# A new instruction order for an adaLN transformer block with local dilated attention and a token-mixing MLP, with the condition first on ScalarE's queue

## The chip, the cores and the metric

The kernel runs on one core of one Trainium2 chip. A core has five engines, each with its own instruction queue worked in order: TensorE (PE, matmuls; PEld is its weight load), VectorE (DVE), ScalarE (ACT), GpSimd (POOL) and SyncE (SP, which here only issues DMA). ACT can issue DMA too. The engines meet at semaphores. The metric is the device time of one execution in microseconds (us).

## What is computed

The reference is one transformer block over 2048 tokens of width 512, modulated by one condition vector `c`:

```python
mod = (silu(c) @ w_mod)            # six rows of 512: sa, ca, ga, sb, cb, gb
h = layernorm(x) * (1 + ca) + sa
x = x + ga * attention(h, wqkv, wo)
h = layernorm(x) * (1 + cb) + sb
x = x + gb * token_mlp(h, w1, b1, w2, b2)
```

The attention has 32 heads of 16 columns. Each token looks at 8 keys at distances 0, 2, ..., 14 before it, and masked positions stand for keys before the first token. The MLP normalizes once more and then mixes along the token axis: `u = gelu(h^T w1 + b1)` with 1792 hidden units for each of the 512 columns, and `y = u w2 + b2` back to 2048 tokens.

## The kernel before

**Tiling.** The 2048 tokens are 16 tiles of 128. Attention goes over them in five chunks of 2, 4, 4, 4 and 2 tiles. In a chunk (function `build_chunk`, from line 616 on) each tile gets its first layernorm: statistics `ln1s`, variance `ln1v`, `rstd1` on ACT, `nb1` on DVE, normalization `n1`. The tiles are then transposed, for the first two chunks by PE (`tr`, with copies `hT` out of the accumulator), later by DMA (`xt`). Twelve or six matmul groups (`qkv`) form q, k and v, and copies (`ev`) take them out. DVE multiplies q with the shifted k (`qk`, one large product for each of four column groups), PE sums these over the head's columns (`red`), and a softmax follows: maximum on DVE (`max`), subtraction on PE (`sub`), exponential on ACT (`exp`), sum on PE (`esum`), reciprocal as two activations on ACT (`rcp`), scaling on DVE (`smB`). The weights are spread to other partitions by DMA (`a2`), v is copied to four shifted layouts by DMA (`vd`), DVE multiplies both (`pv`), PE sums (`pvacc`), ACT copies out (`oev`), and the output projection (`wo`) with the residual gives `x1`. The second layernorm (`ln2`, `n2`, `aff`) and the MLP's own (`ln3`, `h3`) close the chunk.

**The MLP.** The first matrix product (`mlp1`) accumulates over tokens as the chunks finish: for the hidden tiles 0 to 6 in three parts (tiles 0 to 5, 6 to 10, 11 to 15), for 7 to 13 in two (0 to 9, 10 to 15). Parts that are done are parked (`park`) and added back (`padd`), then `gelu` on ACT. The second product (`mlp2`) has 14 matmuls of 512 columns for each of the 16 output tiles; `fin` on DVE adds bias, gate and residual, and `st_out` stores.

**The condition.** `ld_c` loads the vector, PE transposes it with an identity matrix (`cps`), ACT and DVE form silu (`silu_exp`, `silu_dve`), and PE multiplies it with two blocks of `w_mod`: `modcols1` gives the columns of 1 + ca (`a1col`), `modcols0` those of sa (`sab`). `a1col` scales the transposed tokens of the first two chunks (`hT0`, `hT1`) and the qkv weights for the later ones (`wsc`). sa goes through the weights as a bias (`qvb`). The other four rows are formed by `modrow0` and `modrow1` and spread over all partitions by a store and a load (`st_row`, `ld_row`); `woq_s` scales the output projection with ga.

**What sets the order.** Nothing is left to a scheduler at run time. Each piece of work is a node (`add`, `add_any`) with one or more engines it may run on. The string `ORDER` (lines 191 to 249) lists all nodes by name. `schedule` (line 86) walks through it, takes for each node the engine that a suffix names (`:a` ACT, `:d` DVE, `:p` POOL, `:s` SP; on matmuls `:q` splits the stationary operand into four 32-column pieces, `:n` leaves out the matmul that would add a residual or a parked sum), gives it buffers from the pools, and emits its instructions in that order. So the string fixes each engine's instruction order, the order of each DMA queue, and which accumulator buffer each node gets.

**Idle matmuls.** A token `fill:N` emits matmuls of the identity with itself whose result nobody reads: N // 4 of 512 columns and N % 4 of 128 columns (`fill_fn`, line 528). They need only the identity, which POOL makes (`ident`, line 473; its last instruction, the memset of `epscol`, is the one PE waits for). POOL also zeroes the halo (`halo0`) and makes the other constants (`consts`, line 479).

**The names at the front.** `act_table` is ACT's load of its function table. `ld_x0` and `ld_x1` load the first two token tiles of 128 KB each, `ld_x_1_2` and `ld_x_1_4` two pairs of the second chunk, `ld_x_2_6` and `ld_x_2_8` two of the third. `ld_wmod1` and `ld_wmod0` load 512 KB each of `w_mod`, `ld_wqkv0` to `ld_wqkv2` the q, k and v weights. `dma2` (line 381) is a load that may be issued on SP or ACT; `ld_c` is a plain node of ACT in before (lines 429 and 430).

Of the kernel before, what the change touches and what calls it, by code (L numbers as in the profile page):

```python
# [196 lines left out]
qkv0_00 qvb0 wsc0_0:p ev0_10:a ld_b2 ld_wo1 hT1_1:d qkv1_00 ln1s11:d ln1s10:d ln1s13:d qkv1_10:q ln1v11 ln1v10  # L197
qvb_cp0:a ev0_00:a ln1s12:a ev0_02:d qkv1_13 ld_wqkv2 qkv0_20 ln1v13 qk0_3 qk0_2 ev1_13:a qk0_0 qvb1 ln1v12 qkv0_22:q
ld_wrow0 red0_0 ev1_00:a qkv1_03:q ev1_10:a qk0_1 red0_1 red0_2 red0_3 mask qvb_cp1:a ev0_20:a ev0_22:a wsc1_2:p
halo_v1:a qk1_0 ev1_03:a wsc1_3:a qkv1_11:q ld_wmod2 wsc2_3:a modrow0 ld_b1 mrows0:a ev1_11:a ld_wrow2 qkv1_02 max0  # L200
wsc0_2:p ld_wo0 n1_7:p sub0 rstd1_3 qkv1_01 ld_wo2 exp0 qkv1_12:q wsc1_1:p esum0:q qk1_3 red1_0 ev1_01:a qk1_1
ev1_02:a biascols n1_6:p ld_wrow1 rcp0 smB0 ev1_12:a ld_x_4_14 ln1s14:a qkv1_22 qk1_2 a2_0_2:a xt6 ld_wrow3 modrow1
red1_1 a2_0_1:a n1_9:p wsc2_0:d ln1s15:a ln1v14 nb1_3 n1_11:a qkv1_23:q mrows1 qkv1_21 ev1_21:a red1_2 red1_3 xt8
ev1_23:a fill:1 n1_10:p qkv1_20 ev1_20:a ev1_22:a qkv2_13 qkv2_10 wsc0_1:p vd0_2 ev2_13:a ln1v15 vd0_1 max1 sub1
qkv2_00 exp1 a2_0_0:s a2_0_3:s pv0_1 vd0_0 pv0_0 st_row0 pv0_2 qkv2_03 esum1:q ld_wo3 pvacc0_0 vd0_3 halo_v2:p
biascols_cp:a pvacc0_1 pv0_3 pvacc0_2 pvacc0_3 ev2_10:a ev2_00:a qk2_0 n1_13:a n1_12:a ld_row0 woq_s rcp1 smB1
oev0_2:a qkv2_11 qkv2_02:q ev2_03:a qk2_3 qkv2_01:q red2_0 oev0_0:a wo0:q wsc2_1:a wsc2_2:a qkv2_12 ev2_11:a ev2_01:a
ev2_02:a ev2_12:a wo1 qkv2_21:q a2_1_1:a qkv2_22 x1_1:a ln2q1:a x1_0:a xt10 ln2q0:a qk2_1 qkv2_23 xt12 qk2_2 a2_1_0:s
halo_k3:a ln2m0 vd1_2 a2_1_2:s qkv3_12 a2_1_3:s pv1_2 rstd1_4 red2_1 nb1_4 vd1_0 st_row1 red2_2 red2_3 rstd2_0
ev2_22:a nb2_0 ev2_21:a qkv3_13:q ev3_13:a max2 vd1_3 pv1_0 n1_14:a vd1_1 pvacc1_2 n1_15:a qkv2_20:q ev2_20:a sub2  # L210
qkv3_22:q ev3_12:a pv1_1 qkv3_10 exp2 ev2_23:a halo_v3:a qkv3_20 n2_0:a oev1_2:a ev3_10:a esum2 rcp2 qkv3_00 ev3_22:a
qkv3_02:q ev3_00:a pv1_3 ev3_02:a pvacc1_0 ev3_20:a qkv3_01:q ev3_01:a qkv3_11:q xt14 ld_row1 n2_1:p vd2_3 pvacc1_1
smB2 aff0 qk3_0 vd2_1 fill:1 vd2_0 oev1_0:a oev1_1:a pvacc1_3 ev3_11:a qk3_1 qkv3_23:q oev1_3:a a2_2_2:s ln3s1:a
qkv3_03:q wo4 a2_2_1:s qk3_2 a2_2_0:s ev3_03:a ev3_23:a x1_4:a ln2q4:a wo2 x1_2:a a2_2_3:s red3_0 wo3:q x1_3:a ln2q3:a
qkv3_21:q ev3_21:a wo5 red3_1 pv2_3 x1_5:a vd2_2 qk3_3 qkv4_20:q red3_2 qkv4_22 red3_3 qkv4_12 fill:18 ln2q5:a
ld_w1_0_512 ln2q2:a ln2m2 pv2_0 pvacc2_0 vd3_0 ev4_20:a ln3s0:a ln3v0 ev4_12:a rstd2_2 ev4_22:a ln3v1 qkv4_02 oev2_0:a
ln2m4 rstd2_4 nb2_2 n2_2:a max3 sub3:q exp3 pvacc2_3 oev2_3:a qkv4_10:q pv2_2 vd3_2 esum3 nb2_4 pv2_1 vd3_1 n2_3:p
ld_w1_0_0 n2_5:a rcp3 smB3 pvacc2_2 fill:14 a2_3_0:s a2_3_1:s a2_3_3:s n2_4:a qkv4_00:q oev2_2:a rstd3_0 aff2 pvacc2_1
oev2_1:a wo6 wo9 wo7 aff4 nb3_0 ln3s2:d ev4_02:a ln3s3:a ln3v3 h3_1:p wo8 a2_3_2:s ev4_00:a ln3v2 ld_w2_0 ln3s4:d
rstd3_2 nb3_2 x1_9:a ln3s5:a h3_0:p mlp1_0_6_0:q x1_7:a ln3v4 x1_8:a h3_3:d mlp1_0_1_0 h3_2:d mlp1_0_6_2 mlp1_0_1_2  # L220
pv3_1 mlp1_0_5_0:q ln3v5 ev4_10:a ld_w1_0_896 x1_6:a mlp1_0_3_0:q mlp1_0_3_2:q ln2q7:a pvacc3_1 rstd3_4 mlp1_0_5_2:q
oev3_1:a mlp1_0_2_0:q pv3_0 mlp1_0_2_2:q nb3_4 h3_4:a mlp1_0_0_0:q mlp1_0_0_2 h3_5:a mlp1_0_0_4:q qk4_0 ln2q8:a
ln2q6:a park0_0:a ln2q9:a mlp1_0_6_4:q mlp1_0_2_4:q mlp1_0_1_4:q park0_1:a pv3_2 mlp1_0_5_4:q vd3_3 pvacc3_0 oev3_0:a
mlp1_0_3_4:q ld_w2_1 park0_2:a pv3_3 red4_0 ln2m6 pvacc3_2 oev3_2:a mlp1_0_4_0:q qk4_1 pvacc3_3 ld_w1_0_1152
mlp1_0_4_2:q mlp1_0_4_4:q rstd2_6 oev3_3:a wo12:q halo_v4:p vd4_2 vd4_3 nb2_6 n2_9:a qk4_2 n2_7:d qk4_3 wo10:qn red4_1
ld_w1_0_1408 n2_6:a vd4_1 n2_8:a aff6 red4_2 red4_3 max4 park0_3:a ln3s8:d ln3s6:d x1_12:a ln3v8 wo11 vd4_0 ln3s9:d
mlp1_0_7_0 ld_w2_3 park0_4:a ln3v6 mlp1_0_7_2 park0_5:a ln3v9 x1_11:a ln2q12:a mlp1_0_8_0 mlp1_0_8_2 park0_6:a wo13:n
ln3s7:a ln3v7 sub4 mlp1_0_10_0 mlp1_0_9_0 x1_13:d exp4 rstd3_6 nb3_6 esum4 mlp1_0_8_4 ln2q13:a ln2m12 mlp1_0_10_2
mlp1_0_10_4 mlp1_0_9_2 rcp4 mlp1_0_7_4 h3_8:d rstd2_12 mlp1_0_12_0 mlp1_0_12_2 mlp1_0_12_4 smB4 a2_4_1:a a2_4_0:s
mlp1_0_9_4 a2_4_2:s h3_9:d a2_4_3:a h3_7:d nb2_12 h3_6:p mlp1_0_7_6 ln2q11:a park0_7:a x1_10:d mlp1_0_8_6 ld_w1_0_1664  # L230
ln2q10:a park0_8:a n2_13:p mlp1_0_9_6 park0_9:a n2_12:d aff12 ln2m10 rstd2_10 mlp1_0_10_6 park0_10:a ln3s13:a pv4_2
nb2_10 ld_w1_1_0 pv4_1 mlp1_0_11_0 mlp1_0_11_2 mlp1_0_11_4 mlp1_0_12_6 pv4_0 mlp1_0_11_6 ld_w1_1_640 inj1_6:qn pv4_3
pvacc4_0 pvacc4_1 n2_11:a mlp1_0_13_0:q pvacc4_2 pvacc4_3 n2_10:a mlp1_0_13_2:q park0_11:a mlp1_0_13_4 oev4_0:a
oev4_2:a aff10 ln3s10:a wo14 inj1_3:n ln3s11:d ln3v11 x1_14 ln2s14 wo15 x1_15 mlp1_0_13_6 ln2v14 ln3s12:a ln3v10
ln2s15 rstd2_14 nb2_14 ln2v15 n2_14:d rstd3_10 aff14 rstd2_15 nb2_15 inj1_4:qn ln3v13 park0_12:a mlp1_1_3_6 park0_13:a
mlp1_1_6_6 inj1_1:n mlp1_1_1_6 n2_15:p mlp1_1_4_6 inj1_0:n mlp1_1_0_6 nb3_10 h3_10:a mlp1_1_4_10 mlp1_1_3_10 ln3s14:d
# [839 lines left out]
```

## Time and profile before

| what | us |
|---|---|
| median of 3 runs | 201.37 |
| lowest, highest | 201.23, 201.57 |
| profiled execution, whole time | 202.11 |
| its span, first to last instruction | 200.4 |

The granted clock of TensorE is 1.00 over the span. The page slices the span into 40 parts of 5.01 us and gives each engine's busy share in tenths; the last digit for PE is 3 because the last output is formed and stored there:

```profile
PE   3999999999899999999999999999999999999993
PEld 1387754554344455534444444444444444444453
DVE  2689999999999999999999999986655253726554
ACT  4879897998899999999999698953670000000000
POOL 4155001200100001030000200320000000000000
```

PE's digit says that a matmul was in flight, not that it ran at its best pace: matmuls overlap, and one of 512 columns is in flight for 379 to 382 ns in most groups while the next starts behind it much sooner. DVE and ACT digits can be read as they stand. In a row of the timeline the first number is the start, the second the duration; the bracket tells how long the engine was idle before it and who ended that.

### The profile page before, as it was taken

The page shows a single profiled execution, that of the slowest core. Times are in us where ns is not written, and L with a number is a line of the kernel's source. Part 1 is how long each engine was busy: PE and PEld are TensorE (multiplying, and loading weights), DVE is VectorE, ACT ScalarE, POOL GpSimd, SP SyncE. Part 2 cuts the span into 40 slices and gives each one's busy share as a digit, 9 for nine tenths or more (in the row PEclk, how much of TensorE's full clock was granted, in tenths as well). Part 3 has the DMA queues.
Part 4 walks back from the last instruction along what each step waited for, and adds up shares of the span by engine and source line. Part 5 has one row for each costly group of instructions (what it writes and reads, how often), then busy time and mean ns, then how long its engine had stood idle before and what let it go on. Part 6 is the DMA issues. An engine that isn't in the chain of part 4 may idle for free.

```text
span 200.4 us, 4572 instructions
## 1 busy us (share of the span) xinstructions
PE 191.0 (95%) x1818; PEld 95.8 (48%) x1836; DVE 159.6 (80%) x241; ACT 128.6 (64%) x306; POOL 18.6 (9%) x45
## 2 busy tenths in 40 slices
PE   3999999999899999999999999999999999999993
PEld 1387754554344455534444444444444444444453
DVE  2689999999999999999999999986655253726554
ACT  4879897998899999999999698953670000000000
POOL 4155001200100001030000200320000000000000
PEclk9999999999999999999999999999999999999999
DMA  5999594826758745549399268568999201011611
GB/s 161 341 355 350 176 240 127 160 56 185 300 143 321 220 167 194 176 112 311 64 310 257 36 184 196 160 186 234 338 244 298 85 26 52 27 52 52 174 52 52
DMA packets 53889, 35.95 MB, mean 179 GB/s; under 512 B 24428, under 2 KB 50668, under 8 KB 53868
## 3 DMA queue, kind: packets, MB, share of 16 engines
q1 hardware_dynamic: 52228, 35.21, 61.2%
q10 hardware_dynamic: 1640, 0.46, 1.0%
q8 instruction: 14, 0.23, 0.5%
q14 instruction: 7, 0.06, 0.1%
HBM read 22.55 MB, written 2.10 MB: 123 GB/s over the span
## 4 chain that ended last, share of the span: by engine, by line
PE 69%; DVE 22%; issue 4%; DMA 1%; ACT 1%; ACTq 0%; DVEq 0%
PE psS L142 67%; DVE big L142 14%; PE psL L142 3%; DVE st L142 2%; DVE h L142 2%; DMA c_t<-in_c_dram 1%; DVE mv L142 1%; ACT h L142 1%; DVE lsb L142 1%; DVE m L142 1%; DVE nb L142 0%; ACTq L142 0%; DVE woq L142 0%; DVE hT L142 0%; ACT rb L142 0%
## 5 line engine op out<-in xcount | busy, mean ns | idle before, releaser
L142 PEld LDWEIGHTS <-wst 128*128 128x128 bf16 (+1 forms) x536 | 34.9, 101 | 33.7 <-issue 4.0
L142 PE MATMUL psS<-h,wst 128*128 128x512 bf16 (+1 forms) x333 | 50.3, 380 | 0.5 <-issue 0.3
L142 DVE TENSOR_TENSOR big<-q_sb,k_f 128x4096 bf16<-128x4096 bf16 (+1 forms) x20 | 36.6, 1859 | 0.4 <-ACT q_sb L142 0.4
L142 DVE TENSOR_TENSOR big<-a2sb,vD 128x4096 bf16<-128x4096 bf16 (+1 forms) x20 | 36.5, 1860 | 0.2
L142 PE MATMUL psS<-hT,w_qkv 128*32 128x512 bf16 (+3 forms) x360 | 29.7, 346 | 0.0
L142 DVE SCALAR_TENSOR_TENSOR h<-psS,bcol,rows_bc 128x512 f32<-128x512 f32 (+2 forms) x17 | 12.1, 710 | 22.1 <-PE psS L142 20.6
L142 PEld LDWEIGHTS <-w_qkv 128*32 128x32 bf16 (+1 forms) x402 | 19.4, 109 | 17.8 <-issue 4.4
L142 PE MATMUL psS<-gT,big 128*128 128x512 bf16 x110 | 24.7, 379 | 0.1
L142 PEld LDWEIGHTS <-big 128*128 128x128 bf16 x144 | 12.0, 97 | 13.5
L142 ACT ACTIVATE junk<-xx 128x512 bf16<-128x512 bf16 x26 | 16.3, 627 | 3.3 <-DVE xx L142 1.4
L142 PE MATMUL psS<-woq,o_sb 128*32 128x512 bf16 (+1 forms) x107 | 15.7, 380 | 0.9 <-ACT o_sb L142 0.6
L142 ACT ACTIVATE gT<-psS,bcol 128x512 bf16<-128x512 f32 x14 | 9.0, 685 | 8.1 <-DVE psS L142 8.0
L142 POOL TENSOR_SCALAR h<-xx,rs,nb 128x512 bf16<-128x512 bf16 x9 | 6.9, 766 | 75.6 <-DVE nb L142 36.5
L142 DVE TENSOR_TENSOR psS<-psS,gT 128x512 f32<-128x512 f32 x14 | 9.3, 695 | 5.0 <-PE psS L142 5.0
L142 ACT ACTIVATE h<-xx,nb,rs 128x512 bf16<-128x512 bf16 x16 | 12.4, 808 | 0.5 <-DVE nb L142 0.4
L142 PEld LDWEIGHTS <-ident 128*32 128x32 bf16 (+1 forms) x137 | 7.0, 102 | 10.5 <-issue 5.9
L142 PE MATMUL psS<-ident 128*128 128x512 bf16 (+1 forms) x35 | 10.6, 450 | 1.4 <-POOL epscol L142 1.4
L142 PE MATMUL psS<-hT,wst 128*32 128x512 bf16 (+2 forms) x110 | 11.7, 352 | 0.1
L142 DVE TENSOR_TENSOR h<-h,xx 128x512 bf16<-128x512 f32 (+2 forms) x17 | 11.1, 653 | 0.6
L142 DVE TENSOR_TENSOR h<-h,rows_bc 128x1024 bf16<-128x1024 bf16 (+2 forms) x16 | 10.9, 689 | 0.4
L142 DVE BATCH_NORM_STATS2 st<-xx 128x6 f32<-128x512 bf16 x12 | 7.9, 680 | 3.9 <-DMA xx<-in_A_x_dram 3.8
L142 ACT ACTIVATE v_sb<-psS,qvb 128x512 bf16<-128x512 f32 (+1 forms) x20 | 11.0, 595 | 0.0
(100 smaller groups left out, 242.9 us busy)
## 6 DMA issues: line engine op xcount, KB each, us to landing
vD<-v_sb SPq DMA_DIRECT2D x12, 524.5 KB, 4.0
big<-in_B_w_dram SPq DMA_DIRECT2D x4, 896.0 KB, 7.4
...
out_dram<-h SPq DMA_DIRECT2D x15, 128.0 KB, 1.8
...
```

What stands on the lines that cost most here:

```text
L142: r = fn(*a, **k)
```

## The change

There are two edits. The first lets `ld_c` be issued on either queue, like the token tiles; the new order names ACT for it:

```diff
-    add("act", 0.55, lambda: nc.scalar.dma_start(c_t[:], c[0].rearrange("(t p) -> t p", p=P)), writes=["c_t"],
-        name="ld_c", lat=2.0)
+    dma2(c_t[:], c[0].rearrange("(t p) -> t p", p=P), D * 4, ["c_t"], "ld_c")
```

The second replaces the string `ORDER`. It holds the same nodes; only their order, their engine suffixes and the idle matmuls differ. The start and the end of it:

```diff
-ident ld_x_1_2:a halo0 ld_c consts ld_x1:s ld_x0:s ld_x_1_4:s act_table ln1s3:d fill:4 cps ld_wmod1 silu_exp silu_dve
-fill:64 ln1s1:a ln1s2:a ln1s0:d ln1v1 ld_x_2_8 ln1v0 ln1s4:d ld_wqkv0 rstd1_0 nb1_0 n1_1:a fill:4 ln1v4 n1_0:p ln1s5:d
-ln1v2 ln1v5 ln1v3 rstd1_1 nb1_1 ld_x_2_6 modcols1 n1_2:d n1_5:d ln1s8:a a1col wsc0_3:p n1_4:d tr0_0 hT0_1:a hT0_3:a
-n1_3:d hT0_0:a fill:13 hT0_2:a ld_wqkv1 ld_wmod0 ln1s9:d ld_x_3_10 ln1s6:d tr1_0 tr1_2 hT1_2:a ln1v6 qkv0_02 ln1v9
-hT1_0:a qkv0_12 qkv0_10 ln1s7:d ln1v7 ln1v8 rstd1_2 hT1_3:d wsc1_0:a ev0_12:a modcols0 sab:a ld_x_3_12 nb1_2 n1_8:a
...
+act_table ld_c:a ld_x1:s halo0 ld_x0:s ld_x_1_2:a consts ld_x_2_8 ln1s1:d ld_x_1_4:a ln1s0:d ident fill:15 ln1v1 ln1v0
+rstd1_0 ln1s3:d nb1_0 ln1v3 cps ln1s4:d n1_1:p ln1s5:d ln1v4 fill:2 ln1s2:a ln1v2 fill:72 silu_exp ln1v5 rstd1_1
+silu_dve ln1s8:a ld_wmod1 nb1_1 n1_2:d modcols1 ld_x_2_6 a1col n1_5:d ld_wqkv1 n1_4:d n1_0:p wsc1_3:p tr0_0 hT0_1:a
+fill:8 ld_wqkv0 wsc1_0:p hT0_0:a fill:5 n1_3:d tr1_2 ld_wmod0 wsc1_2:p hT0_2:a ln1s7:d hT0_3:a wsc0_2:p hT1_3:a
+wsc1_1:d ln1s9:d ld_x_3_10 ln1s6:d ln1v9 tr1_0 ld_x_3_12 ld_wo2 qkv0_12 hT1_2:a qkv0_02 ln1v7 hT1_0:a ln1v8 ln1v6
...
+st_out14_0 fin13_0 st_out13_0 mlp2_15_0 fin15_0 st_out15_0 mlp2_15_1 fin15_1 st_out15_1 mlp2_15_2 fin15_2 st_out15_2
+fill:20
```

What it moves, as far as the prediction speaks of it:

- The idle matmuls: `fill` 4, 64, 4 and 13 at the front, 1, 1, 18 and 14 in the middle become 15, 2, 72, 8 and 5 at the front, 28, 4 and 6 in the middle and 20 at the end.
- POOL: `halo0` and `consts` stand ahead of `ident`.
- ACT's queue begins with `act_table`, `ld_c`, `ld_x_1_2`, `ld_x_1_4`; in before it began with `ld_x_1_2`, `ld_c`, `act_table`.
- SP's queue: `ld_x1 ld_x0 ld_x_2_8 ld_wmod1 ld_x_2_6 ld_wqkv1 ld_wqkv0 ld_wmod0`, in before `ld_x1 ld_x0 ld_x_1_4 ld_wmod1 ld_x_2_8 ld_wqkv0 ld_x_2_6 ld_wqkv1 ld_wmod0`. Later `ld_w2_1` stands ahead of the fourth chunk's `a2_3` transfers and `ld_w1_0_896` between the second chunk's `vd1_1` and `vd1_3`.
- Nodes with another engine: `ln1s1`, `ln1s12` and `ln2q10` from ACT to DVE; `qvb_cp0` from ACT to DVE; `wsc1_1`, `n2_13` and `n2_15` from POOL to DVE; `hT1_1`, `hT1_3`, `ev0_02`, `h3_8`, `n2_14` and `ln3s14` from DVE to ACT; `h3_7` from DVE to POOL; `n1_6`, `n1_7`, `wsc0_0`, `halo_v2`, `halo_v4` and `h3_12` from POOL to ACT; `n1_1`, `n1_12`, `wsc1_0`, `wsc1_3`, `halo_v1`, `halo_v3`, `h3_10` and `h3_11` from ACT to POOL; `a2_1_1` and `a2_4_3` from ACT's queue to SP's.
- On DVE, `n1_5` stands behind `a1col` (ahead of it in before), `woq_s` ahead of the first chunk's `pv` products (behind them in before), and the four `qk` and `pv` products of most chunks are in another order among themselves.

More of the change, by code (lines that the diff above doesn't have):

```diff
@@ L197 @@
[L197 to L236, printed above, removed]
@@ new lines @@
+fill:8 ld_wqkv0 wsc1_0:p hT0_0:a fill:5 n1_3:d tr1_2 ld_wmod0 wsc1_2:p hT0_2:a ln1s7:d hT0_3:a wsc0_2:p hT1_3:a
+wsc1_1:d ln1s9:d ld_x_3_10 ln1s6:d ln1v9 tr1_0 ld_x_3_12 ld_wo2 qkv0_12 hT1_2:a qkv0_02 ln1v7 hT1_0:a ln1v8 ln1v6
+rstd1_2 qkv0_10 modcols0 nb1_2 wsc0_3:p ln1s11:d ld_b2 ev0_12:a hT1_1:a ld_wqkv2 ln1s10:d sab:a qkv0_00 n1_7:a qvb0
+ln1s12:d ld_wmod2 ln1v10 qkv1_10 ev0_10:a qkv1_13 qvb_cp0:d ev0_00:a ln1s13:d qkv1_00 qvb1 n1_8:a n1_6:a ev0_02:a
+qkv0_20 ln1v11 ln1v12 ev1_00:a ln1v13 ld_wrow3 qk0_1 rstd1_3 qk0_0 ld_wrow1 modrow0 wsc0_1:p qk0_3 qkv0_22:q ev1_13:a
```

60 lines of the change are left out of this document (48 added, 12 removed).

## Prediction

> **What bounds the kernel now.** I read the page first, then busy time by stretch, the chain of waits, and the timeline of the first 13 us, because that is where the diff moves most.
>
> ```profile
> span 200.4 us, 4572 instructions
> PE 191.0 (95%) x1818; PEld 95.8 (48%) x1836; DVE 159.6 (80%) x241; ACT 128.6 (64%) x306; POOL 18.6 (9%) x45
> ```
>
> The averages hide three stages. Two stretches separate the last two, and a few steps of the chain show which engine carries each:
>
> ```profile
> 20.00:110.00 90.00, 87.73 (x1209) 44.62 (x1217) 88.95 (x99) 84.47 (x205) 5.23 (x8) 1.00 0.69 196
> 104.00:197.30 93.30, 92.59 (x491) 43.81 (x499) 63.25 (x119) 34.77 (x82) 4.57 (x6) 1.00 0.54 147
> ```
>
> ```profile
> 0.82 0.48 ACTq L142
> ...
> 1.33 2.60 DMA c_t<-in_c_dram
> ...
> 11.10 0.16 DVE a1col L142
> ...
> 133.85 10.95 PE psS L142 x50
> ...
> 188.02 9.31 PE psS L142 x70
> ```
>
> The columns of the stretches are length, then PE, weight loads, DVE, ACT, POOL. From 20 to 110 us DVE is busy 88.95 of 90 us: it is the bound, and only 1.05 us of gaps can be won there. ACT, with 84.47 of 90, is close behind. From 104 us PE takes over and has no gap worth naming up to 197 us. Ahead of both stands the front: the condition lands at 3.93, a row of idle matmuls and the column matmuls run to 11.06, then DVE forms `a1col` and its own chain begins. A delay of `a1col` therefore pushes DVE, and DVE pushes PE: front time is worth its full price as long as DVE stays full.
>
> The front in detail (start, duration, engine):
>
> ```profile
> 2.94 0.29 POOL L142 TENSOR_SCALAR_AFFINE_SELECT nident<-nident 128x128 bf16<-128x128 bf16 x1
> ```
>
> ```profile
> 1.43 0.61 PE L142 MATMUL psS<-ident 128*128 128x512 bf16 x1 [1.43 <-POOL epscol L142]
> 3.98 0.18 PE L142 MATMUL psS<-ident,c_t 4*128 4x4 bf16 x1 [1.94 <-DMA c_t<-in_c_dram]
> 4.10 6.58 PE L142 MATMUL psS<-ident 128*128 128x512 bf16 x17
> 10.52 0.54 PE L142 MATMUL psS<-sc,big 128*128 128x1 bf16 x16
> ```
>
> ```profile
> 9.19 0.15 PEld L142 LDWEIGHTS <-ident 128*128 128x128 bf16 x1 [0.28 <-issue]
> 9.62 0.57 PEld L142 LDWEIGHTS <-ident 128*128 128x128 bf16 x3 [0.28 <-issue]
> ```
>
> ```profile
> 9.70 0.74 DVE L142 TENSOR_SCALAR h<-xx,rs,nb 128x512 bf16<-128x512 bf16 x2
> 11.10 0.16 DVE L142 TENSOR_SCALAR a1col<-psS 128x4 f32<-128x4 f32 x1 [0.66 <-PE psS L142]
> ```
>
> PE starts when POOL has `ident`; it waits for the condition; then 17 idle matmuls of 512 columns follow at 0.43 us each (9.62 - 9.19) and the column matmuls stand behind them at 10.52. Near 9.7 us the pace changes: seventeen at 0.43 would last 7.3 us and not 6.58, and later matmuls of that width take 10.95 / 50 = 0.22 us. DVE waits 0.66 us for `a1col`.
>
> **The change part by part: the front.** POOL now makes `ident` last of its constants. The same instructions run in another order, so PE starts at 2.94 + 0.29 = 3.23 instead of 1.43. On ACT's queue the table load moves ahead of the three DMAs:
>
> ```profile
> 1.33 0.61 ACTq L142 DMA_DIRECT2D c_t<-in_c_dram  x1
> 1.98 1.28 ACT L142 ACT_TABLE_LOAD   x1 [1.98 <-issue]
> ...
> 46.73 0.60 ACT L142 ACTIVATE k_f<-psS 128x512 bf16<-128x512 f32 x1
> 46.79 0.62 ACTq L142 DMA_DIRECT2D a2sb<-lsb  x1
> ```
>
> The DMA at 46.79 was issued while an activation ran, so an issue need not wait for ACT's work in hand; whether it may pass a table load no row shows. The ends: issued at 0.8, landed at 0.8 + 2.6 = 3.4; or issued at 0.8 + 1.28 = 2.1, landed at 4.7. Neither decides, because `fill:15` (three matmuls of 512 columns, three of 128) covers 3.23 + 3 x 0.43 + 3 x 0.11 = 4.85 (a quarter of the width at a quarter of the time). The condition's transpose therefore comes at 4.85, not 3.98. Were that cover gone, the later landing would cost up to 0.7.
>
> Behind it stand `fill:2` and `fill:72`: 0.2 us and 18 matmuls of 512 columns from 5.1 on. All at the slow pace they would last 18 x 0.43 = 7.7 (`a1col` +2.3), all at the fast one 18 x 0.22 = 4.0 (-1.4). The switch near 9.7 came 5.7 us after PE's unbroken run began at 3.98. The same lag from 3.23 gives 8.9: nine slow matmuls to 8.95, nine fast ones to 10.9. The column matmuls then start at 10.9 instead of 10.52: **+0.4**. If the switch stayed at 9.7 by the clock, eleven slow and seven fast end at 11.3: +0.75. I take +0.4, the row's own lag.
>
> [...]
>
> DVE does not hold the front. This is the landing of the first pair of token tiles, then come the groups of DVE's short instructions, with count, busy time and mean ns:
>
> ```profile
> xx<-in_A_x_dram SPq DMA_DIRECT2D x2, 128.0 KB, 2.2
> ```
>
> ```profile
> L142 DVE BATCH_NORM_STATS2 st<-xx 128x6 f32<-128x512 bf16 x12 | 7.9, 680 | 3.9 <-DMA xx<-in_A_x_dram 3.8
> L142 DVE TENSOR_SCALAR h<-xx,rs,nb 128x512 bf16<-128x512 bf16 x7 | 3.2, 480 | 0.0
> L142 DVE TENSOR_SCALAR hT<-psS,a1col 128x512 bf16<-128x512 bf16 x2 | 1.0, 478 | 0.0
> L142 DVE TENSOR_TENSOR q_sb<-psS,qvb 128x512 bf16<-128x512 f32 x1 | 0.7, 692 | 0.2 <-ACT qvb L142 0.2
> L142 DVE TENSOR_SCALAR w_qkv<-h,a1col 128x512 bf16<-128x512 bf16 x1 | 0.3, 346 | 0.0
> ```
>
> In before it sat idle for 3.8 us until its first tokens had landed, and then reached `a1col` at 10.44 (9.70 + 0.74). The new list ahead of `a1col` has `ln1s1` more (0.68) and `n1_5` less (0.48): 10.6 by the same start. It now begins with the pair on SP's queue, which lands 2.2 us after its issue at 0.8, so 0.8 sooner: 9.8, against 11.5 for `a1col`. The two token pairs on ACT's queue may land as much as a table load (1.3) later; the 1.7 between hides that. Behind the waiting `a1col` stand three normalizations on DVE (two in before), the `wsc` scalings on POOL and the four `hT0` copies on ACT, as before; all go with it.
>
> **DVE from `a1col` on.** Its list up to the third softmax gains `n1_5` 0.48, `ln1s12` 0.68, `wsc1_1` 0.35 and a copy of four columns (0.16, as `a1col`), 1.67 in all; it loses `hT1_3` and `hT1_1` at 0.48 and `ev0_02` at 0.69, 1.65. Sum: nothing. The products `qk`, `pv` only change places inside their chunk. What can change is gaps.
>
> **ACT's list before the first softmax ends is longer.** DVE's `smB0` needs `rcp0`:
>
> ```profile
> 29.74 0.26 ACT L142 ACTIVATE rb<-ls 128x64 bf16<-128x64 f32 x1
> ```
>
> ```profile
> 31.14 0.42 DVE L142 TENSOR_TENSOR lsb<-lsb,rb 128x512 bf16<-128x512 bf16 x1
> ```
>
> ```profile
> L142 ACT ACTIVATE junk<-xx 128x512 bf16<-128x512 bf16 x26 | 16.3, 627 | 3.3 <-DVE xx L142 1.4 <-issue 1.4
> L142 ACT ACTIVATE h<-xx,nb,rs 128x512 bf16<-128x512 bf16 x16 | 12.4, 808 | 0.5 <-DVE nb L142 0.4
> L142 ACT ACTIVATE q_sb<-psS,qvb 128x256 bf16<-128x256 f32 x6 | 2.5, 466 | 0.0
> L142 ACT ACTIVATE w_qkv<-h,a1col 128x512 bf16<-128x512 bf16 x3 | 2.0, 721 | 0.0
> L142 ACT ACTIVATE hT<-psS,a1col 128x512 bf16<-128x512 bf16 x2 | 1.3, 684 | 0.3 <-PE psS L142 0.3
> ```
>
> ```profile
> 12.00:30.00 18.00, 17.80 (x292) 12.52 (x294) 17.09 (x27) 16.55 (x42) 5.10 (x8) 1.00 0.98 270
> ```
>
> The margin is 31.14 - 30.00 = 1.14. Ahead of `rcp0` come in addition two `hT1` copies (1.4), `n1_6` and `n1_7` (1.6), `ev0_02` (0.8 to 0.9) and one scaling (0.7); three scalings (2.1) and the small `qvb_cp0` and `halo_v1` (0.4) go, while one statistics pair and one `ev1` swap for their like. Net 2.0 to 2.1. If none of it falls into ACT's gaps, DVE stalls 2.1 - 1.14 = 0.95 at `smB0`; ACT has 18 - 16.55 = 1.45 of gaps there, and if they take it, 0. Below 0 the bound is the 1.05 us of gaps that DVE has now. I take **+0.3**, a third of the stall, since the gaps are larger than what is left over but each of them ends at a wait of its own. Later softmaxes keep a longer ACT list; a stall taken once moves DVE back for them.
>
> **PE's end.** Behind `pv4_3`, the last attention product, PE has the same matmuls left in either order. DVE reaches it 0.4 us of work later (`n2_13` 0.48 and `ln2q10`, about 0.75, come in; `h3_8` and `h3_7`, normalizations too, leave):
>
> ```profile
> 118.17 2.35 DVE L142 TENSOR_TENSOR big<-a2sb,vD 128x2048 bf16<-128x2048 bf16 x2
> ...
> 120.56 0.61 PE L142 MATMUL psS<-big,group 128*32 128x256 bf16 x16
> ```
>
> The products end at 120.52 and PE takes the last one at 120.56, coming straight from other matmuls: 0 if PE is as late as DVE, 0.4 if not. I take **+0.2**.
>
> **At nothing:** the other idle matmuls. In mid-kernel there are 38 units of 128 columns instead of 34, 0.2 us of PE in a stretch where DVE is the bound; the 20 at the very end last five times 0.22 = 1.1 us after PE's last product, while the output is still being formed and stored (PE ends near 197.3, the span at 200.4). On SP's queue a weight load now stands ahead of the exchange of the fourth softmax (`ld_w2_1`) and one between the second chunk's `vD` loads (`ld_w1_0_896`); `vD` lands 4.0 us after issue, and two products of 2.29 lie ahead of the first that needs it:
>
> ```profile
> vD<-v_sb SPq DMA_DIRECT2D x12, 524.5 KB, 4.0
> ```
>
> ```profile
> L142 DVE TENSOR_TENSOR big<-a2sb,vD 128x4096 bf16<-128x4096 bf16 x12 | 27.2, 2286 | 0.1
> ```
>
> If that cover went, each would cost an issue slot, about 0.5.
>
> **Sum:** 0.4 + 0.3 + 0.2 = 0.9 us. The profiled execution took 202.11 (span 200.4 and 1.7 around it); it would become 203.0. The runs without a profile have a median of 201.37, 0.74 below it, so the time to expect is 201.37 + 0.9 = **202.3**.
>
> **Rivals.**
>
> A, *the clock rises earlier* (faster). PE's run starts 0.75 earlier; if the rise came half as late behind its start as in the row (2.85, so at 6.1), two slow and sixteen fast matmuls end at 9.5, and `a1col` stands 0.6 behind, at 10.1: -1.0. For it speaks that nothing in the trace ties the rise to the number of matmuls. Against it, the only lag shown is 5.7. ACT and PE's end give back some 0.3 of it: 201.37 - 0.7 = 200.7. [...]
>
> B, *the gaps pay for the front* (no change). DVE's work is the same to 0.1, so a front of +0.4 vanishes if the new order closes 0.4 of its 1.05 us of gaps and ACT's list hides: 201.4. Against it: the gaps are many and small.
>
> C, *ACT becomes the bound* (slower by more). If ACT's gaps absorb nothing, DVE waits 0.95 at `smB0`, and the clock's rise fixed at 9.7 adds 0.75, PE's end 0.4: 2.1, so 203.5. It decides once ACT's list ahead of `rcp0` ends later than DVE's.
>
> D, *the change doesn't do what it says*: the condition stands first among ACT's transfers but behind the table load, so it may be issued at 2.1, later than the 1.33 of before. `fill:15` hides that, so the time is the forecast's; it is part of its chance.
>
> **How the numbers follow.** Forecast 0.46 (own range 201.8 to 203.0), A 0.21, B 0.17, C 0.16. A measurement of this kernel tells about 0.2% (0.4 us) from no change. Faster is A and a little of B: 0.23; the same is most of B: 0.15; slower is the rest: 0.62. The range goes from 200.6, just beyond A, to 203.5, C's sum.
>
> **What would show it.** In the profile of after: PE's first matmul near 3.2; the condition's matmul near 4.9; column matmuls near 10.9 and DVE's wait for `a1col` of 0.9 us or more; a gap of DVE ahead of `smB0` (128x512, lsb) ended by ACT; from 20 to 110 us DVE busy 88.5 or less of 90. Wrong would be: column matmuls before 10 (A), DVE gaps smaller than 0.7 there (B), or a first condition matmul later than 5.5, which no step above foresees. If the end moves though `a1col` does not, the front was not the cause.

## The result, and the profile after

The changed kernel takes 203.77 us in the median (202.63 to 204.17) against 201.37 (201.23 to 201.57) before: slower, by a ratio of 1.0101 with a 95% interval of 1.0075 to 1.0127, which is about 2.0 us (the two medians lie 2.40 apart). The forecast was slower by 0.9. Its profiled execution took 204.17 with a span of 201.7.

The page of after, first two lines:

```profile
span 201.7 us, 4670 instructions
PE 192.5 (95%) x1869; PEld 96.9 (48%) x1886; DVE 159.7 (79%) x242; ACT 126.8 (63%) x303; POOL 19.4 (10%) x45
```

Busy time by stretch, after (length, then PE, weight loads, DVE, ACT, POOL):

```profile
20.00:110.00 90.00, 87.90 (x1248) 44.50 (x1255) 89.11 (x95) 84.46 (x205) 5.89 (x8) 1.00 0.73 200
104.00:197.30 93.30, 92.70 (x531) 43.44 (x529) 62.65 (x117) 36.01 (x85) 4.59 (x6) 1.00 0.51 141
```

From 20 to 110 us DVE is as full as before (89.11 against 88.95), and PE as full from 104 on. The loss is not a lasting wait inside these stretches; it lies ahead of them, in small pieces along DVE's list, and behind the last instruction. The front of after, in the timeline (start, duration, engine):

```profile
0.81 1.28 ACT L142 ACT_TABLE_LOAD   x1 [0.81 <-PEq L1060]
0.84 0.57 ACTq L142 DMA_DIRECT2D c_t<-in_c_dram  x1
...
3.27 1.78 PE L142 MATMUL psS<-ident 128*128 128x512 bf16 x6 [3.27 <-POOL epscol L142]
4.98 0.18 PE L142 MATMUL psS<-ident,c_t 4*128 4x4 bf16 x1
...
8.65 1.82 PEld L142 LDWEIGHTS <-ident 128*128 128x128 bf16 x9 [0.23 <-issue]
...
10.81 0.54 PE L142 MATMUL psS<-sc,big 128*128 128x1 bf16 x16
11.39 0.16 DVE L142 TENSOR_SCALAR a1col<-psS 128x4 f32<-128x4 f32 x1 [1.27 <-PE psS L142]
11.46 1.81 DVE L142 TENSOR_SCALAR h<-xx,rs,nb 128x512 bf16<-128x512 bf16 x3
```

The front went as forecast: PE starts at 3.27, the condition's matmul comes at 4.98 and the column matmuls at 10.81, 0.29 behind before. The condition's transfer was issued at 0.84, while the table load ran (0.81 to 2.09). The weight loads of the idle matmuls, 0.43 us apart until then, close up from 8.65 on: that is where the pace changes.

Three later marks on DVE's list are the scalings of the first and of the last softmax (`lsb`) and DVE's last instruction. After:

```profile
31.73 0.42 DVE L142 TENSOR_TENSOR lsb<-lsb,rb 128x512 bf16<-128x512 bf16 x1
...
112.50 0.42 DVE L142 TENSOR_TENSOR lsb<-lsb,rb 128x512 bf16<-128x512 bf16 x1
...
198.25 0.29 DVE L142 TENSOR_TENSOR h<-psS,fpre 128x128 bf16<-128x128 f32 x1
```

Before (the first scaling, at 31.14, is shown with the prediction):

```profile
111.58 0.43 DVE L142 TENSOR_TENSOR lsb<-lsb,rb 128x512 bf16<-128x512 bf16 x1
...
197.36 0.29 DVE L142 TENSOR_TENSOR h<-psS,fpre 128x128 bf16<-128x128 f32 x1
```

With these marks every profile of this study can be cut into the same five pieces. The columns are: when PE's unbroken run of matmuls begins; where the pace changes, about; start of `a1col`; from there to the first softmax's scaling; from that to the last softmax's; from that to the start of DVE's last instruction; from the end of that instruction to the end of the span; the span. Spans are printed to 0.1, so the column before the span is good to 0.05. Run names are those of the experiments below.

| kernel | PE from | pace | a1col | to first | to last | to DVE's last | to the end | span |
|---|---|---|---|---|---|---|---|---|
| before | 3.98 | 9.7 | 11.10 | 20.04 | 80.44 | 85.78 | 2.75 | 200.4 |
| trail_added | 3.87 | 6.9 | 10.24 | 20.03 | 80.46 | 85.77 | 2.71 | 199.5 |
| front_fill_grown | 4.13 | 8.9 | 11.61 | 20.04 | 80.46 | 85.77 | 2.73 | 200.9 |
| before_fill_cut | 3.98 | none by 9.2 | 10.35 | 20.60 | 80.44 | 85.77 | 2.75 | 200.2 |
| before_pool_short | 3.87 | 8.6 | 10.50 | 20.01 | 80.46 | 85.79 | 3.25 | 200.3 |
| **after** | 3.27 | 8.7 | 11.39 | 20.34 | 80.77 | 85.75 | 3.16 | 201.7 |
| no_trail | 3.26 | 8.8 | 11.44 | 20.36 | 80.75 | 85.61 | 3.15 | 201.6 |
| norm_ahead | 3.25 | 8.8 | 11.48 | 19.65 | 81.57 | 85.61 | 3.20 | 201.8 |
| a2_sync | 3.27 | 9.2 | 11.67 | 20.37 | 80.89 | 85.61 | 3.17 | 202.0 |
| act_lighter | 3.25 | 7.3 | 10.86 | 19.90 | 80.77 | 85.75 | 2.83 | 200.4 |
| front_fill_cut | 3.26 | 8.0 | 10.53 | 19.91 | 81.54 | 85.61 | 3.22 | 201.1 |
| ident_early | 1.43 | 5.6 | 10.73 | 19.91 | 82.35 | 85.76 | 3.46 | 202.5 |
| early_a2_sync | 1.44 | 6.4 | 10.80 | 19.61 | 80.83 | 85.61 | 3.96 | 201.1 |
| after_mended | 1.44 | 5.2 | 10.21 | 19.66 | 81.25 | 85.60 | 3.09 | 200.1 |

Two things are to be seen. In the kernels made from before, the span is `a1col` + 189.3 within 0.05 (189.8 in the two kernels that change something behind it). In the changed kernel and two others with its front, no_trail and a2_sync, it is `a1col` + 190.2 to 190.3. So behind an `a1col` as late as in these three the new order costs 1.0. And the `a1col` of a profile is one draw: with nearly the same front it came at 10.24, 10.50 and 11.10 in kernels made from before.

### The profile page after: what moved, and what is told of

Read it like the earlier page. It is cut to its first block, busy times and chain, and to the rows that moved or that the text cites. A ratio compares the mean times of both kernels' runs of the same rounds, so it can differ in the third digit from the quotient of the medians.

```text
span 201.7 us, 4670 instructions
## 1 busy us (share of the span) xinstructions
PE 192.5 (95%) x1869; PEld 96.9 (48%) x1886; DVE 159.7 (79%) x242; ACT 126.8 (63%) x303; POOL 19.4 (10%) x45
## 4 chain that ended last, share of the span: by engine, by line
PE 70%; DVE 21%; issue 5%; POOL 1%; ACT 1%; DVEq 0%; POOLq 0%
PE psS L142 68%; DVE big L142 14%; DVE h L142 3%; PE psL L142 2%; DVE m L142 1%; DVE lsb L142 1%; DVE mv L142 1%; DVE st L142 1%; ACT q_sb L142 0%; DVE nb L142 0%; POOL group L142 0%; ACT lsb L142 0%; POOL ident L142 0%; POOL mask L142 0%; POOL nident L142 0%
## 5 line engine op out<-in xcount | busy, mean ns | idle before, releaser
L142 PE MATMUL psS<-woq,o_sb 128*32 128x512 bf16 (+1 forms) x121 | 16.2, 380 | 0.8 <-ACT o_sb L142 0.7
L142 PE MATMUL psS<-ident 128*128 128x512 bf16 (+1 forms) x46 | 12.2, 420 | 3.3 <-POOL epscol L142 3.3
L142 PEld LDWEIGHTS <-ident 128*32 128x32 bf16 (+2 forms) x175 | 8.0, 101 | 11.8 <-issue 4.6
L142 ACT ACTIVATE h<-xx,nb,rs 128x512 bf16<-128x512 bf16 x17 | 13.4, 812 | 0.3 <-DVE nb L142 0.2
L142 ACT ACTIVATE junk<-xx 128x512 bf16<-128x512 bf16 x21 | 13.2, 627 | 0.3
L142 ACT ACTIVATE q_sb<-psS,qvb 128x512 bf16<-128x512 f32 (+1 forms) x20 | 11.4, 600 | 2.7 <-PE psS L142 2.6
L142 DVE BATCH_NORM_STATS2 st<-xx 128x6 f32<-128x512 bf16 x14 | 9.2, 682 | 4.8 <-DMA xx<-in_A_x_dram 4.8
L142 ACT ACTIVATE v_sb<-psS,qvb 128x512 bf16<-128x512 f32 (+1 forms) x20 | 11.5, 599 | 0.3 <-PE psS L142 0.2
L142 ACT ACTIVATE junk<-h 128x512 bf16<-128x512 bf16 x18 | 11.4, 631 | 0.3
```

Source lines behind the costliest of these rows:

```text
L142: r = fn(*a, **k)
```

## The experiments

The times of before, beside which each was measured, were 201.43, 201.71 and 201.53 in the medians of the three groups of runs. These are the changed kernel and its variants beside them:

| kernel | median | ratio to before (95% interval) |
|---|---|---|
| after | 203.77 | 1.0101 (1.0075 to 1.0127) |
| no_trail | 203.45 | 1.0085 (1.0065 to 1.0106) |
| front_fill_cut | 203.19 | 1.0083 (1.0056 to 1.0111) |
| ident_early | 203.64 | 1.0096 (1.0070 to 1.0122) |
| early_a2_sync | 202.91 | 1.0061 (1.0039 to 1.0083) |
| a2_sync | 203.33 | 1.0094 (1.0061 to 1.0126) |
| norm_ahead | 203.36 | 1.0078 (1.0051 to 1.0105) |
| act_lighter | 203.25 | 1.0068 (1.0043 to 1.0094) |

The interval of every variant overlaps that of after. So no time in this table tells a variant from after by itself; what an edit did is read from its profile.

### The idle matmuls at the end

no_trail is the changed kernel without them:

```diff
-fill:20
```

> The changed kernel without the idle matmuls at its very end (fill:20, five matmuls of 512 columns). Theory, the end pays for them: in the changed kernel the last of them ends at 199.29 us, 0.75 after VectorE's last instruction (198.54), and 3.16 us lie between that instruction and the end of the span, against 2.75 in the kernel before (197.65 to 200.4). Without them 0.4 should come off the span, and up to 0.7 more off what lies outside it (2.47 in the changed kernel's profiled run, 1.71 before): 202.7 to 203.4 against 203.77, and 2.75 from VectorE's last instruction to the end. Rival, the prediction's: they are hidden while the output is stored: 203.77 within 0.2, and still 3.1 to 3.2 from VectorE's last instruction to the end.

trail_added is the kernel before with them:

```diff
 ... st_out15_2
+fill:20
```

> The kernel before with those five idle matmuls of 512 columns put at its end, and nothing else. Theory, the end pays for them: 0.4 to 1.1 more than 201.37, so 201.8 to 202.5, and 3.1 or more from VectorE's last instruction to the end of the span. Rival, hidden behind the stores: 201.37 within 0.2.

Measured: no_trail 203.45 (202.77 to 203.64), and 3.15 us from DVE's last instruction to the end, as in after. trail_added 201.24, ratio 0.9993 (0.9978 to 1.0007), and 2.71. The time of no_trail lies between the two ranges that were expected and decides nothing; the unchanged end and trail_added do. The idle matmuls are hidden, as the prediction had it; the theory that they are paid at the end fell. The longer end of after has another cause.

### The length of the front

front_fill_cut (changed kernel) and front_fill_grown (kernel before):

```diff
-... fill:72 ...
+... fill:56 ...
```

> The changed kernel with fill:56 in place of fill:72, four idle matmuls of 512 columns less ahead of the column matmuls. Their last nine ran at 0.20 to 0.22 us each, so a1col should come 0.87 earlier, at 10.5 instead of 11.39, if the change of pace stays near 8.7. Theory, the front carries its full price because VectorE is full from there on: 203.77 - 0.9 = 202.9, with VectorE's last instruction 0.9 earlier as well. Rival, another wait takes its place in the front (statistics, normalizations, q and k products) or the gaps of VectorE take it: 203.5 to 203.8 with a1col early.

```diff
-... fill:64 ...
+... fill:80 ...
```

> The kernel before with fill:80 in place of fill:64, four idle matmuls of 512 columns more ahead of the column matmuls. a1col should come 0.87 later, near 11.97 instead of 11.10. Theory, the front carries its full price: 201.37 + 0.9 = 202.25. Rival, the gaps of VectorE (1.05 us between 20 and 110) take it: 201.4 to 201.7.

front_fill_grown took 202.32, 0.9 more than 201.43 (ratio 1.0040, 1.0016 to 1.0064): DVE's gaps give nothing back. Its `a1col` came at 11.61 and not near 11.97, since the pace changed at 8.9 and not at 9.7 as in the profile of before. Its timeline, beside that of trail_added, shows it (`a1col`, first scaling, last instruction of each):

```profile
11.61 0.16 DVE L142 TENSOR_SCALAR a1col<-psS 128x4 f32<-128x4 f32 x1 [1.03 <-PE psS L142]
...
31.65 0.42 DVE L142 TENSOR_TENSOR lsb<-lsb,rb 128x512 bf16<-128x512 bf16 x1
...
197.88 0.29 DVE L142 TENSOR_TENSOR h<-psS,fpre 128x128 bf16<-128x128 f32 x1
```

```profile
10.24 0.16 DVE L142 TENSOR_SCALAR a1col<-psS 128x4 f32<-128x4 f32 x1
...
30.27 0.42 DVE L142 TENSOR_TENSOR lsb<-lsb,rb 128x512 bf16<-128x512 bf16 x1
...
196.50 0.29 DVE L142 TENSOR_TENSOR h<-psS,fpre 128x128 bf16<-128x128 f32 x1
```

The 1.37 between the two `a1col` is 1.38 at the first softmax and 1.38 at the last instruction.

front_fill_cut took 203.19, 0.6 less than 203.77 and not the 0.9 expected. Its DVE:

```profile
10.53 0.16 DVE L142 TENSOR_SCALAR a1col<-psS 128x4 f32<-128x4 f32 x1
10.61 1.35 DVE L142 TENSOR_SCALAR h<-xx,rs,nb 128x512 bf16<-128x512 bf16 x3
...
30.44 0.42 DVE L142 TENSOR_TENSOR lsb<-lsb,rb 128x512 bf16<-128x512 bf16 x1
...
41.95 2.29 DVE L142 TENSOR_TENSOR big<-q_sb,k_f 128x4096 bf16<-128x4096 bf16 x1 [0.67 <-ACT q_sb L142]
```

`a1col` is 0.86 earlier and the first softmax even 1.29, since the three normalizations take 1.35 instead of 1.81. In these profiles a normalization took DVE 0.40 to 0.42 where it began before GpSimd's first scaling of weights, and 0.71 to 0.79 where it began while one ran. In after GpSimd starts at 11.65 and the second and third begin at 11.79 and 12.50; here it must wait for its weights,

```profile
10.96 4.35 POOL L142 TENSOR_SCALAR w_qkv<-wst,a1col 128x512 bf16<-128x512 bf16 x6 [3.56 <-DMA wst<-in_A_wqkv_dram]
```

and the second still begins ahead of it, at 10.93. But at 41.95 DVE waits 0.67 for ACT, and at the second softmax the lead is down to 0.54 (44.22 against 44.76). ACT had stood still for 1.71 at the issue of a transfer:

```profile
33.83 0.63 ACTq L142 DMA_DIRECT2D a2sb<-lsb  x1
34.50 0.69 ACT L142 ACTIVATE v_sb<-psS,qvb 128x512 bf16<-128x512 f32 x1 [1.71 <-PE psL L142]
```

This is the wait that ident_early shows below and early_a2_sync removes. So in before a later front is handed on in full, while in the changed order an earlier one meets another chain.

before_fill_cut, the kernel before with less:

```diff
-... fill:64 ...
+... fill:48 ...
```

> The kernel before with fill:48 in place of fill:64, four idle matmuls of 512 columns less ahead of the column matmuls. Theory, the time of the kernel before spreads because the pace of TensorE changes at another time in each execution (9.7 in its profile, 6.85 and 8.9 in two kernels with the same front): with less work ahead of the column matmuls a1col waits for VectorE alone, near 10.25, in every execution: spans of 199.3 to 199.6, 201.1 in the median, and less spread. Rival, the shorter run of idle matmuls leaves TensorE slow behind a1col: 201.4 or more.

It took 201.28 against 201.71, ratio 0.9981 (0.9967 to 0.9996), so it beats both kernels by a little. As the theory had it, `a1col` comes at 10.35 without a wait of DVE. In the profiled execution PE was still at its slow pace ahead of the column matmuls, and the stretch to the first softmax took 20.60 instead of 20.04; but that is not the rival's doing. From 10.53 on PE's idle matmuls run at the quick pace, four of 512 columns in 0.87, and DVE waited 1.1 us for token tiles:

```profile
12.06 0.69 DVE L142 BATCH_NORM_STATS2 st<-xx 128x6 f32<-128x512 bf16 x1 [0.31 <-DMA xx<-in_A_x_dram]
...
16.19 1.88 DVE L142 BATCH_NORM_STATS2 st<-xx 128x6 f32<-128x512 bf16 x3 [0.78 <-DMA xx<-in_A_x_dram]
```

trail_added, whose `a1col` came as early, has neither wait. Why the tiles landed later here, no run shows.

### What the front waits for

ident_early:

```diff
-act_table ld_c:a ld_x1:s halo0 ld_x0:s ld_x_1_2:a consts ld_x_2_8 ln1s1:d ld_x_1_4:a ln1s0:d ident fill:15 ...
+act_table ld_c:a ld_x1:s ident halo0 ld_x0:s ld_x_1_2:a consts ld_x_2_8 ln1s1:d ld_x_1_4:a ln1s0:d fill:31 ...
```

> The changed kernel with the identity made ahead of GpSimd's other constants and fill:31 in place of fill:15 (four idle matmuls of 512 columns more), so that TensorE runs without a break from 1.44 instead of 3.27 and comes to the condition's transpose at the same time, 4.9. Theory A, the matmuls change pace some 2.9 to 5.7 us after TensorE's unbroken run began (the lags of the runs so far): the change of pace comes 1.8 earlier, near 4.4 to 7.1, the column matmuls are ready by 9.5 and a1col waits for VectorE alone, near 10.2 instead of 11.39: 203.77 - 1.2 = 202.6. Rival, the pace changes at a time that has nothing to do with the start of TensorE's run: a1col stays near 11.4 and the time at 203.6 to 203.9.

203.64: no gain to speak of, and yet theory A was right about the pace. PE starts 1.8 sooner, the pace changes 4.1 behind that as in act_lighter, and `a1col` comes 0.66 earlier, though not the 1.2 expected:

```profile
5.55 3.33 PEld L142 LDWEIGHTS <-ident 128*128 128x128 bf16 x16 [0.24 <-issue]
...
10.15 0.54 PE L142 MATMUL psS<-sc,big 128*128 128x1 bf16 x16 [0.77 <-DVE sc L142]
...
10.73 0.16 DVE L142 TENSOR_SCALAR a1col<-psS 128x4 f32<-128x4 f32 x1
```

PE now waits for DVE (`sc`), the silu of the condition, which the new order puts behind the statistics of the pair that lands last. And the lead of 1.09 at the first softmax (30.64) was lost behind it. ACT in the same run, and SP's queue:

```profile
32.36 0.72 ACT L142 ACTIVATE w_qkv<-h,a1col 128x512 bf16<-128x512 bf16 x1
34.88 0.62 ACTq L142 DMA_DIRECT2D a2sb<-lsb  x1
35.55 0.69 ACT L142 ACTIVATE v_sb<-psS,qvb 128x512 bf16<-128x512 f32 x1 [2.46 <-PE psS L142]
```

```profile
28.39 1.54 SPq L142 DMA_TRANSPOSE hT<-h  x1
```

The wait of 2.46 is put down to PE, which had long been done. ACT stood at the issue of a transfer (34.88): that instruction waits on a counter of finished transfers which the transposing transfer of 28.39 counts up too, and the trace has that transfer's last count at 34.86. front_fill_cut and norm_ahead show the same: the last count came at 33.80 and 34.57, the issue at 33.83 and 34.59. In after the counter was full at 32.27, and the issue came at 33.37 without a wait.

early_a2_sync tests this: ident_early with the transfer on SP's queue.

```diff
-... nb1_3 vd0_0 a2_0_1:a ev1_21:a ...
+... nb1_3 vd0_0 ev1_21:a ...
-qkv2_12 a2_0_0:s woq_s ...
+qkv2_12 a2_0_0:s a2_0_1:s woq_s ...
```

> The kernel of the run ident_early with one transfer of the first chunk's exchange, a2_0_1, on SyncE's queue behind a2_0_0 instead of ScalarE's. In ident_early VectorE ended the first softmax at 31.06, 1.09 ahead of the changed kernel, and yet ended its last instruction 0.49 later (199.04): ScalarE stood still for 2.46 us ahead of the issue of a2_0_1 (34.88). Theory, that issue waits for a counter of finished transfers that it shares with the transposing transfer issued at 28.39 on SyncE, and the wait delays ScalarE's normalization for the next chunk: with the transfer on SyncE the lead of about 1.1 stays, VectorE ends near 197.5 and the time is 203.64 - 1.5 = 202.1 (up to 0.4 more, since the loads of vD are issued 0.65 later). Rival, ScalarE waited there for something else (its matmuls, or the chunk's data): it waits at the next instruction, and the time stays at 203.3 to 203.8.

Measured 202.91. The second softmax's scaling, at 45.26 in ident_early, shows the wait gone:

```profile
30.41 0.42 DVE L142 TENSOR_TENSOR lsb<-lsb,rb 128x512 bf16<-128x512 bf16 x1
...
43.44 0.68 DVE L142 TENSOR_TENSOR lsb<-lsb,rb 128x1024 bf16<-128x1024 bf16 x1
...
196.85 0.29 DVE L142 TENSOR_TENSOR h<-psS,fpre 128x128 bf16<-128x128 f32 x1
```

DVE's last instruction ends at 197.14, 1.9 ahead of ident_early, where 197.5 was expected. The median gained only 0.73 of the 1.5 expected: in the profiled execution 3.96 lay behind DVE's end, 0.80 more than in after, and one of the last stores took 1.16 to issue, where in after they took 0.33 to 0.38; why, no run shows.

a2_sync is the same edit on the changed kernel alone:

> The changed kernel with a2_0_1 on SyncE's queue behind a2_0_0 and nothing else. In its own profile ScalarE did not wait for this issue (33.37), so the wait can only show in executions in which the front is early. Theory: 0.1 to 0.5 less than 203.77, 203.3 to 203.7, with more of the early executions left (spans under 201). Rival, the wait plays no part in the changed kernel itself, or the loads of vD behind it cost as much: 203.6 to 204.0.

203.33 (ratio 1.0094, 1.0061 to 1.0126). It lies where the theory puts it, but the interval overlaps almost all of that of after; this does not tell the two apart. The spans under 201 that the theory also expected did not come: the two shortest are 201.0.

### What stands behind a1col

norm_ahead:

```diff
-n1_2:d modcols1 ld_x_2_6 a1col n1_5:d ...
+n1_2:d n1_5:d modcols1 ld_x_2_6 a1col ...
```

> The changed kernel with the normalization n1_5 ahead of a1col on VectorE instead of behind it; nothing else moves. In the changed kernel VectorE waits 1.27 us for a1col (11.39) and then forms three normalizations in 1.81 us, two of them at 0.7 because GpSimd scales weights beside them, where the one ahead of a1col takes 0.41. Theory, what is behind a1col is late: n1_5 fits into the wait, so 0.35 to 0.45 come off everything behind it, VectorE's third from a1col to the end of the first softmax included: 203.77 - 0.4 = 203.4. Rival, another wait of the front (statistics, the weights' scaling) takes its place: 203.77 within 0.15.

203.36, next to the 203.4 expected, but partly by luck. Its DVE:

```profile
11.48 0.16 DVE L142 TENSOR_SCALAR a1col<-psS 128x4 f32<-128x4 f32 x1 [1.06 <-PE psS L142]
11.55 1.11 DVE L142 TENSOR_SCALAR h<-xx,rs,nb 128x512 bf16<-128x512 bf16 x2
...
31.13 0.42 DVE L142 TENSOR_TENSOR lsb<-lsb,rb 128x512 bf16<-128x512 bf16 x1
...
44.98 0.69 DVE L142 TENSOR_TENSOR lsb<-lsb,rb 128x1024 bf16<-128x1024 bf16 x1
```

The stretch to the first softmax falls from 20.34 to 19.65, by 0.69: a normalization of 0.79 behind `a1col` became one of 0.41 in a wait. That is more than the 0.35 to 0.45 expected. In this execution ACT then lost 1.76 at the same shared counter, and the stretch to the last softmax grew by 0.80 (81.57 against 80.77), which nobody had expected.

act_lighter:

```diff
-... n1_7:a ...
+... n1_7:p ...
-... n1_6:a ...
+... n1_6:p ...
```

> The changed kernel with the normalizations n1_6 and n1_7 on GpSimd instead of ScalarE, which takes 1.6 us off ScalarE's list ahead of the reciprocal of the first softmax. Rival C of the prediction, ScalarE decides at the first softmax: 0.3 to 0.9 come off, 202.9 to 203.5. Theory from the trace of the changed kernel (the reciprocal ended at 31.29, VectorE was busy until 31.82): ScalarE does not decide, 203.77 within 0.3, or a little more where GpSimd slows VectorE beside it. It also changes GpSimd's list by two instructions: if the 0.35 us that GpSimd loses between two semaphore instructions at the end of the program (200.65 to 201.07, where the kernel before has 199.72 to 199.80) hang on the length of its list, the stretch between VectorE's last instruction and the end of the span falls from 3.16 to 2.8.

203.25 lies where rival C was expected (202.9 to 203.5), but the profile speaks against C. In it the stretch to the first softmax is 19.90, just as in front_fill_cut (19.91) and ident_early (19.91), where ACT has its full list and `a1col` is as early: taking 1.6 off ACT changed nothing there, and rival C falls. The end, though, is 2.83 instead of 3.16:

```profile
197.28 0.29 DVE L142 TENSOR_TENSOR h<-psS,fpre 128x128 bf16<-128x128 f32 x1
```

### The end of the program

before_pool_short:

```diff
-... h3_13:p ...
+... h3_13:a ...
-... h3_14:p ...
+... h3_14:a ...
```

> The kernel before with the last two normalizations of GpSimd (h3_13, h3_14) on ScalarE, which is busy for 20.4 of the 77 us there; nothing else moves. GpSimd's list becomes two instructions shorter, as that of the changed kernel is. Theory, the 0.35 us that GpSimd loses at the end of the program hang on where its list ends: 3.1 instead of 2.75 from VectorE's last instruction to the end of the span, 201.43 + 0.35 = 201.8. Rival, they belong to something else in the changed kernel's order: 2.75, and 201.4 within 0.15.

201.88 against 201.53 (ratio 1.0010, 0.9994 to 1.0027), with 3.25 from DVE's end to the end of the span (200.3) instead of 2.75:

```profile
196.76 0.29 DVE L142 TENSOR_TENSOR h<-psS,fpre 128x128 bf16<-128x128 f32 x1
```

The time alone is just short of telling; the profile is clear. Among GpSimd's last seven instructions, semaphore instructions and drains 0.03 to 0.08 us apart, one gap is about 0.35 longer in some kernels: in after it is the one from 200.67 to 201.07, in before_pool_short it is one instruction later, in act_lighter, before and its kin there is none. So it moves when normalizations change between GpSimd and ACT; both lists change in these runs, and neither was varied alone. The length of GpSimd's list in instructions is not the rule by itself: after_mended has as many as before and still has the gap, four instructions later. What decides the place stays open.

### All places mended

after_mended takes the edits of ident_early (with `fill:48` for `fill:72`), early_a2_sync, norm_ahead, act_lighter and no_trail, and moves the silu ahead of the late statistics:

```diff
-cps ln1s4:d n1_1:p ...
+cps silu_exp silu_dve ln1s4:d n1_1:p ...
```

> The changed kernel with all the places mended that the runs so far point to: the identity first and fill:31, fill:48 for fill:72, the condition's exponential and its four small operations directly behind its transpose, n1_5 ahead of a1col, a2_0_1 on SyncE's queue, n1_6 and n1_7 on GpSimd, no idle matmuls at the end. Theory, these places are the whole of the difference: a1col at 10.3 to 10.9, the first softmax ended near 30.4, VectorE's last end near 196.9, 2.8 from there to the end of the span: 199.7, and 1.7 around it: 201.4 (201.1 to 201.9), the kernel before within its spread. Rival, the order behind the first softmax is slower by itself or another wait appears: 202.3 or more.

201.91 (ratio 1.0008, 0.9986 to 1.0029): the kernel before within what can be measured, though 0.5 behind the 201.4 expected. Its DVE:

```profile
10.21 0.16 DVE L142 TENSOR_SCALAR a1col<-psS 128x4 f32<-128x4 f32 x1
...
29.87 0.42 DVE L142 TENSOR_TENSOR lsb<-lsb,rb 128x512 bf16<-128x512 bf16 x1
...
36.52 4.63 DVE L142 TENSOR_TENSOR big<-a2sb,vD 128x2048 bf16<-128x2048 bf16 x4 [0.36 <-DMA a2sb<-lsb]
...
196.72 0.29 DVE L142 TENSOR_TENSOR h<-psS,fpre 128x128 bf16<-128x128 f32 x1
```

The first softmax is 1.86 earlier than in after; then a wait for the exchange takes 0.36 back, and the end has its 0.35 again. So the time is back at that of before, but not because every loss is gone. Against the 10.5 that the next section takes as typical for before, `a1col` is 0.3 earlier, the stretch behind it is 0.38 shorter and the one behind the last softmax 0.18; the middle is still 0.81 longer and the end 0.34. The mended places pay for the rest. The version to keep is still the kernel before, or before_fill_cut.

## Why the prediction was right or wrong

The direction was right. The ratio puts the time at 201.37 x 1.0101 = 203.4, at the upper end of the range; the median of after itself, 203.77, is 0.27 beyond it. The sum of five pieces, after against a typical execution of before, is 1.05 + 0.30 + 0.33 - 0.03 + 0.41 = 2.06, and 2.03 was measured (201.37 times 0.0101). The 1.05 of the front is worked out from the spans, so that the sum meets their difference is no proof of it. The profiles give it a second time: `a1col` came at 10.24, 10.50 and 11.10 with the front of before, at 10.86, 11.39, 11.44, 11.48 and 11.67 with that of after, 0.94 apart in the middle.

That the time came out inside the range was in part luck. Of the three terms of the sum two measured nothing, and about half of the loss lies in places that were put at nothing. C's sum of 2.1 is nearest to what was measured, though its mechanism did not occur. Of the signs named, those of the front came: PE's first matmul at 3.27, the condition's at 4.98, the columns at 10.81 and a wait of 1.27 for `a1col`. A gap ahead of `smB0` did not come, and DVE was busy 89.11 and not 88.5 or less.

- **The front, forecast +0.4.** The mechanism was right: PE starts later, has more matmuls ahead of the columns and changes pace on the way. With the row's own lag of 5.7 the columns were to start at 10.9, and they started at 10.81; that this execution's lag was 5.4 is luck, since act_lighter with the same front had 4.1. The size was not right, because the row was no typical one. Spans of before run from 199.2 to 200.7, with 199.8 in the middle; its profile has 200.4. If span = `a1col` + 189.3 holds for all of them, the middle is an `a1col` of 10.5, not the 11.10 of the profile. For after, 201.85 - 190.3 = 11.55: +1.05. The step that failed is the last of the sum: the 0.74 between the profiled execution and the median was carried along as a constant, while most of it was, by these spans, a late change of pace, a thing the change acts on. In before `a1col` stands against DVE's own list whenever the pace changes early (10.24, no wait); in after PE's unbroken run has four more idle matmuls of 512 columns ahead of the columns (21 against 17), and in four of the five profiles with this front `a1col` waits for PE.
- **DVE's list up to the first softmax, forecast 0.** Measured +0.30. The count of work was right; the durations were not. The instructions of tile `h` in after up to 13.5 us (shortest, median and longest in ns):

```profile
L142 DVE TENSOR_SCALAR h<-xx,rs,nb x4: 404/596/791, 9.7 to 12.5; 128x512 bf16<-128x512 bf16 x4
```

  Two of the four are the slow kind, beside GpSimd; before has one (11.50, 0.79), so the new order pays 0.38 more. The step that failed is "`n1_5` less (0.48)" ahead of `a1col` and the same 0.48 behind it: in after a normalization took 0.41 at 9.70 and 0.79 at 11.79. With an early `a1col` the new order is 0.13 shorter here than the old one (19.91 against 20.04).
- **ACT's stall ahead of `smB0`, forecast +0.3.** Measured nothing. The reciprocal in after:

```profile
31.04 0.26 ACT L142 ACTIVATE rb<-ls 128x64 bf16<-128x64 f32 x1
```

  It ends at 31.30, 0.43 ahead of the scaling at 31.73: of the margin of 1.14, 0.71 is used up, so ACT's gaps took most of the 2.1. act_lighter shows that ACT does not decide there.
- **PE's end, forecast +0.2.** Measured -0.03 (85.75 against 85.78 from the last softmax on).
- **At nothing:** right for the idle matmuls at the end. What was costed at nothing and was not: the middle of DVE's list, +0.33, which no experiment tested. Nearly all of it, 0.30, lies between the scalings of the third and the fourth softmax: 21.71 or 21.72 in the five kernels made from before, 22.02 or 22.03 in the nine with the new order. In after 0.09 of this is work of DVE (21.64 against 21.55) and the rest small gaps between short instructions. The other is the end of the program, +0.41, of which 0.35 is GpSimd's gap. Neither was foreseen. Of the transfers' new places the price was seen only where the first softmax came early (31.13 or before): an issue on ACT's queue then waited for a transfer of SP's queue (ACT idle for 1.71, 1.76 and 2.46).
- **Rivals.** A asked for an earlier change of pace behind an earlier start of PE; ident_early shows that the start does pull the change along, but the lag of 2.85 that A needed came in no profile with the front of after (4.1 to 5.9). B fell with front_fill_grown: gaps pay for nothing. C named the wrong engine. D did not hold: the condition was issued at 0.84, earlier than the 1.33 of before.

The lag from the start of PE's unbroken run to the change of pace was 3.0 (trail_added) to 5.9 us (a2_sync) over the profiles that show the change; what sets it, no run shows. Ahead of the lag of 3.0 a single matmul had run at 1.44, but so it had in every kernel with the front of before. What the prediction calls the rise of the clock the traces show as a change of pace: in before a matmul of 512 columns is in flight for 0.63 us ahead of it and 0.38 behind it, and the granted clock is 1.00 on both sides.
